# A table of its own for the last batch, and the tail casts of batch 0 on VectorE

## The chip, the cores and the metric

One Trainium2 chip, one of its cores. The metric is the device time of one execution in microseconds, the median of several runs; lower is better.

## The reference

Eight batches, each with 8 heads, 576 positions and 64 values a head. First a retention layer, then a gated layer with a spatial product (all in float32):

```
scores = q @ k^T / 8;  ret = scores * Dmat          # Dmat = gamma_h ** (i - j) for i >= j, else 0
x      = ret @ v                                     # per head; heads side by side: (8, 576, 512)
h      = relu(x @ w_in)                              # w_in 512 x 1024
u, v   = h[..., :512], h[..., 512:]
v_n    = (v - mean(v)) / sqrt(var(v) + 1e-6)
v_s    = einsum('ts,bsd->btd', w_spatial, v_n) + b_spatial[None, :, None]
out    = (u * v_s) @ w_out                           # w_out 512 x 512
```

## The kernel before

**Numbers.** Each fp32 operand of the three large products is kept as a rounded part and a remainder (hi and lo, type fp32r), and a product is three matmuls. ScalarE (ACT) writes hi with a copy or cast, VectorE (DVE) or GpSimd (POOL) writes lo with a subtraction. The weights arrive as 64-bit words and are taken apart by a chain of seven steps: ACT absolute value; maximum on DVE or POOL; shift, high word, low word on DVE, with a PSUM bank as scratch; ACT hi; lo on DVE or POOL.

**Stages.** The 576 positions of a batch are four chunks of 128 and a tail of 64. For each chunk: scores, mask, state update with two decays (dec1 and dec0), and a burst of matmuls that gives a chunk of x. The tail's 64 positions are collected in a tile `xt` and must then be put into the places of the tail in x (`place`). For batches 0 and 1 this is two casts SBUF to SBUF, one for hi and one for lo. From x follow the v half of h with its normalisation (`v`), the u half, the spatial product with the gate, and the output product. Batches 0 and 1 use plain products (`PLAIN = 2`), because the weights are still being made; batches 2 to 7 use a scheme with seven instead of eight products of quarter blocks, whose sums and splits are more DVE, ACT and POOL work.

**Order.** Each engine runs its instructions in program order, and the program order is written out by hand: the tables `ORDER` (start, batches 0 and 1, and the attention of the next ones) and `STEADY` (once for each of the batches 2 to 7, with a, b, c standing for the batch and the two after it; names of batches that don't exist are left out). Each word names a chain, and each time that it stands in the table the chain does its next step. The letters that matter here:

- `w.kind.i.xy` weight block (kind 1: v half of w_in, 0: u half, 2: w_out), maximum on x, lo on y (p POOL, v DVE); `s.n.x` block of w_spatial, lo on x
- `d.b.c`, `D.kind.i`, `T.b`, `S`, `c.x` loads, all issued from the SP queue; `z` a matmul on zeros that only keeps TensorE (PE) busy; `m` two fills on POOL
- `k.b.c.x`, `q.b.c.x` scalings of k and q on x; `g` scores and mask; `p.b.c.xy` state update with dec1 on x and dec0 on y; `b` the burst of a chunk; `t.b.x` and `e.b.x` the tail, prepared and placed on x
- `v.b.n` v half and normalisation of chunk n (4: the tail); a third field says which engine takes the maximum with 0
- `U.t` the first u product of batch 0, 12 matmuls, for columns `t`; `V`, `G`, `X` spatial products and gates; `F` output products
- `W.b.kind.m.part` quarter-block products of batches 2 to 7 (A is three products one after the other in one bank, each copied out by ACT; B two products; C and E one); `R`, `K`, `Y`, `Z` the splits and sums for them

**PSUM.** Four banks are free for all products. Which one a chain takes is read from the string `BANKS`, in order of first use; a chain waits until the last reader of the bank before it is done. The `v` chains of batch 0 keep their bank from the first matmul to the last DVE step of the normalisation. In batches 2 to 7 v lies in the tile `u` in SBUF, and the u half later overwrites its rows.

The steps that the change speaks of:

```
def tail_end(b, eng=po):
    ...
    place_tail(b, eng)          # b < PLAIN: for i in range(2): eng.tensor_copy(out=tail_places(xs[b][:, i]), in_=halves[i])
def decay(t, s, eng=po):
    eng.tensor_tensor(out=t, in0=s, in1=sd.broadcast_to([P, NP, D]), op=ALU.mult)
```

Of the kernel before, what the change touches and what calls it, by code (L numbers as in the profile page):

```python
# [977 lines left out]
```

## Time and profile before

| | us |
|---|---|
| median of 3 runs | 519.97 |
| lowest, highest | 516.78, 521.62 |
| the profiled execution | 519.32 |
| its span, first to last instruction | 517.5 |
| PE busy in the span | 499.2 (96%) |
| DVE, ACT, POOL busy | 403.5, 244.8, 164.6 |

Busy time of PE comes from records in which matmuls overlap, so 96% busy is not 96% of the peak. An engine's idle time matters only where the work that ends last goes through it. Nearly every instruction is recorded under line 166, the helper through which all engines are called, so the rows are told apart by operation and tiles: `out<-in` with buffer numbers left out.

### The profile page before, as it was taken

The numbers are of one execution on the slowest core, as the hardware profiler recorded it, in microseconds if no ns is written. First come the engines' busy times: TensorE is split into PE (matmuls) and PEld (weight loads), VectorE is DVE, ScalarE is ACT, GpSimd is POOL, SyncE is SP. The second block draws the span as 40 slices with busy tenths as digits, with TensorE's granted clock in tenths as the row PEclk, the third lists the DMA queues.
The fourth block names the chain that finished last, engine by engine and source line by source line (L and its number), as shares of the span: only waits on it lengthen the run. The fifth ranks groups of instructions, "written<-read, shape, count | busy, mean of one in ns | idle before, by whom it ended". The sixth has DMA issues, their size and how long they took to land.

```text
span 517.5 us, 16958 instructions
## 1 busy us (share of the span) xinstructions
PE 499.2 (96%) x7323; PEld 471.7 (91%) x7323; DVE 403.5 (78%) x878; ACT 244.8 (47%) x521; POOL 164.6 (32%) x146
## 2 busy tenths in 40 slices
PE   6897999999999999999999999999999999999996
PEld 4676899899999999999999999999999999998996
DVE  3998687997799976788669786888768885877654
ACT  2466516545345462537326472446426472356322
POOL 2796344433016540236014250234213350131010
PEclk9997999999999999999999999999999999999999
DMA  8994343033505522152223442053222420020002
GB/s 282 406 315 164 104 135 116 9 107 103 162 24 156 166 88 84 41 186 84 62 84 106 127 140 80 17 167 129 63 84 67 159 85 1 2 92 1 1 1 92
DMA packets 29949, 55.53 MB, mean 107 GB/s; under 512 B 3249, under 2 KB 15793, under 8 KB 29618
## 3 DMA queue, kind: packets, MB, share of 16 engines
q1 hardware_dynamic: 29874, 54.45, 32.1%
q8 instruction: 57, 0.93, 0.8%
q14 instruction: 18, 0.15, 0.1%
HBM read 45.00 MB, written 9.44 MB: 105 GB/s over the span
## 4 chain that ended last, share of the span: by engine, by line
PE 81%; DVE 10%; DMA 3%; issue 2%; ACT 2%; POOL 1%; SPq 0%; DVEq 0%; ACTq 0%; POOLq 0%
PE m L166 69%; PE r L166 11%; DVE u L166 4%; DMA lent_slot<-in_w_in 2%; DVE slot L166 2%; DVE dec L166 1%; ACT slot L166 1%; DVE m L166 1%; DMA out<-o 1%; ACT u L166 0%; ACT m L166 0%; DVE kn L166 0%; DVE lent_vn L166 0%; POOL room L166 0%; DVE sm L166 0%
## 5 line engine op out<-in xcount | busy, mean ns | idle before, releaser
L166 PE MATMUL m<-wsp,vn 128*128 128x288 f32 x768 | 113.4, 296 | 0.6 <-issue 0.6
L166 PEld LDWEIGHTS m<-wsp,vn 128*128 128x128 f32 x768 | 105.2, 188 | 1.4 <-issue 0.7
L166 DVE TENSOR_TENSOR u<-m,u 128x288 f32<-128x288 f32 (+1 forms) x104 | 45.2, 436 | 21.4 <-PE m L166 12.3
L166 POOL TENSOR_TENSOR slot<-u,slot 128x576 fp32r<-128x576 f32 x8 | 11.5, 1435 | 140.9 <-ACT slot L166 140.9
L166 PE MATMUL m<-slot,win 128*128 128x288 f32 x336 | 53.2, 306 | 2.6 <-DVE vn L166 2.6
L166 PEld LDWEIGHTS m<-slot,win 128*128 128x128 f32 x336 | 49.2, 198 | 3.4 <-POOL wtl L166 3.0
L166 ACT COPY u<-m 128x288 f32<-128x288 f32 (+1 forms) x78 | 28.7, 381 | 32.0 <-PE m L166 26.6
L166 DVE SCALAR_TENSOR_TENSOR u<-u,m 128x288 f32<-128x288 f32 x48 | 21.1, 450 | 28.8 <-PE m L166 28.4
L166 PE MATMUL m<-slot,wout 128*128 128x288 f32 x264 | 39.4, 295 | 0.0
L166 PEld LDWEIGHTS m<-slot,wout 128*128 128x128 f32 x264 | 36.4, 188 | 0.5 <-issue 0.2
L166 PE MATMUL m<-win,slot 128*128 128x512 f32 (+1 forms) x168 | 36.0, 350 | 0.0
L166 ACT CAST slot<-u 128x576 fp32r<-128x576 f32 x32 | 21.5, 674 | 25.8 <-DVE u L166 25.7
L166 ACT COPY r<-warm 1x2 f32<-1x2 f32 x32 | 4.9, 152 | 56.9 <-PE r L166 56.7
L166 PEld LDWEIGHTS m<-win,slot 128*128 128x128 f32 x168 | 26.9, 188 | 4.1
L166 PE MATMUL m<-quarter,slot 128*128 128x256 f32 x216 | 29.9, 283 | 0.5 <-ACT u L166 0.5
L166 POOL TENSOR_TENSOR qk<-qk,qs 128x512 f32<-128x512 f32 (+1 forms) x18 | 23.2, 1286 | 22.4 <-PE r L166 15.1
L166 PE MATMUL m<-slot,part 128*128 128x288 f32 x168 | 27.9, 302 | 2.1 <-ACT o L166 1.5
L166 ACT CAST places<-u 128x576 fp32r<-128x576 f32 x21 | 14.2, 678 | 31.4 <-DVE u L166 31.1
L166 POOL TENSOR_TENSOR kn<-kn,kd 128x512 f32<-128x512 f32 x17 | 17.8, 1048 | 34.1 <-DMA kn<-in_qkv 29.7
L166 PEld LDWEIGHTS m<-quarter,slot 128*128 128x128 f32 x216 | 27.0, 188 | 1.1 <-ACT u L166 0.7
L166 PE MATMUL m<-wtl,vt 128*128 128x288 f32 (+1 forms) x128 | 27.5, 296 | 0.4 <-DVE vt L166 0.4
L166 PEld LDWEIGHTS m<-slot,part 128*128 128x128 f32 x168 | 23.6, 188 | 4.5 <-ACT o L166 2.6
(167 smaller groups left out, 1218.9 us busy)
## 6 DMA issues: line engine op xcount, KB each, us to landing
qk<-in_qkv SPq DMA_DIRECT2D x30, 512.0 KB, 4.3
kn<-in_qkv SPq DMA_DIRECT2D x30, 256.0 KB, 5.0
vv<-in_qkv SPq DMA_DIRECT2D x30, 256.0 KB, 4.4
out<-o SPq DMA_DIRECT2D x32, 144.0 KB, 1.9
tail<-in_tails SPq DMA_DIRECT2D x8, 384.0 KB, 3.3
lent_slot<-in_w_in SPq DMA_DIRECT2D x4, 512.0 KB, 7.0
raw<-in_w_in SPq DMA_DIRECT2D x4, 512.0 KB, 11.5
raw<-in_w_out SPq DMA_DIRECT2D x4, 512.0 KB, 5.9
```

The costliest lines, as they stand in the source:

```text
L166: ins = op(*args, **kw)
```

## The change

- **A third table, `LAST`,** is run for batch 7 in place of `STEADY`. It holds the same steps of batch 7 in another order. The maximum of `v.7.0` goes from DVE to ACT, `Y.7.1` (lo) from DVE to POOL and `Y.7.2` from POOL to DVE.
- **`ORDER`** has the same steps in another order up to about the third chunk of batch 1; from there to its end each engine's order is the old one. These change their engine: `e.0` (the two casts) POOL to DVE; `t.1` and `k.0.2`, `k.1.3`, `q.0.0` POOL to DVE; the maximum of `w.2.1` POOL to DVE; lo of `w.0.1` DVE to POOL; dec1 of `p.0.0` and dec0 of `p.0.0` change places (DVE has dec1); dec0 of `p.0.1` and `p.1.1` DVE to POOL; dec1 of `p.1.0` DVE to POOL. (`e.1` was on DVE before.)
- **`STEADY`** is interleaved anew, with the same steps on the same engines.
- **`BANKS`** is a new string of the same length.

Around the v chains of batch 0, DVE's order before was: v.0.1 statistics steps, dec1 of p.1.0, the four small steps of v.0.2, last step of v.0.1, add of v.0.4, last step of v.0.2. It becomes: the small steps of v.0.1 and v.0.2, last step of v.0.1, the two casts of e.0, add of v.0.4, last step of v.0.2. PE's order there was v.0.4, v.0.3 v0 to v2, b.1.0, v.0.3 v3, U.1, U.0; it becomes v.0.4 and v.0.3 in turns, b.1.0, v.0.3 v2 and v3, U.1, U.0.

The diff, cut to its core:

```
 ORDER = """
-    D.1.1 z.29.1 m c.d z.0.1 c.k z.14.1 d.0.0 z.15.1 c.a d.0.0 z.27.1 d.0.0 z.17.1 c.q z.1.1 z.21.1 z.28.1 z.25.1
-    D.1.3 z.3.1 w.1.1.vp z.13.1 D.1.0 z.7.1 w.1.1.vp d.0.1 d.0.1 g.0.0 d.0.1 g.0.0 D.1.2 k.0.0.v w.1.1.vp d.0.2
...
-    p.0.3.pp S v.0.0 t.0.p t.0.p b.0.2 S v.0.1 w.0.1.pv g.0.3 s.0.p b.0.2 w.0.0.pp p.0.2.pp w.0.1.pv v.0.1 q.0.3.p
...
-    b.0.3 k.1.0.p g.1.0 d.1.2 b.0.3 d.1.1 w.0.2.pv s.4.p D.2.1 v.0.2 s.1.p v.0.0 D.0.3 e.0.p p.1.0.vv e.0.p v.0.2
-    w.0.2.pv s.3.v v.0.4 s.0.p d.1.2 v.0.2 b.0.3 v.0.4 d.1.2 v.0.1 v.0.4 b.0.3 q.1.1.p v.0.4 v.0.1 p.1.0.vv v.0.3
-    v.0.2 p.1.0.vv v.0.3 s.2.p s.5.p v.0.3 v.0.1 v.0.4 e.0.p b.1.0 v.0.2 v.0.3 k.1.1.p v.0.1 v.0.2 v.0.4 U.1 s.5.p
...
+    D.1.1 z.16.1 d.0.0 z.14.1 c.a z.22.1 c.k z.0.1 d.0.0 d.0.0 z.8.1 c.q z.15.1 D.1.3 z.17.1 z.3.1 z.2.1 z.13.1 c.d
+    w.1.1.vp w.1.1.vp w.1.1.vp D.1.0 g.0.0 d.0.1 g.0.0 d.0.1 k.0.0.v d.0.1 D.1.2 p.0.0.vp q.0.0.v d.0.2 w.1.1.vp
...
+    D.2.0 e.0.v k.1.0.p w.0.2.pv v.0.2 s.3.v e.0.v v.0.2 w.0.2.pv s.1.p s.5.p p.1.0.pv w.0.2.pv b.0.3 v.0.4 v.0.2
+    d.1.2 b.0.3 s.0.p s.2.p v.0.3 d.1.2 v.0.2 D.2.1 p.1.0.pv v.0.4 d.1.1 v.0.1 q.1.1.p v.0.2 v.0.3 D.0.3 v.0.2 v.0.4
+    T.1 v.0.1 s.2.p v.0.4 v.0.1 b.1.0 v.0.4 v.0.3 e.0.v v.0.2 p.1.0.pv v.0.3 v.0.4 s.4.p k.1.1.p v.0.2 U.1 v.0.4
+    b.1.0 v.0.4 s.5.p p.1.0.pv U.0 U.1 v.0.4 s.4.p v.0.4 v.0.3 s.3.v b.1.0 g.1.1 b.1.0 d.1.3 p.1.0.pv p.1.1.pp b.1.0
...
+LAST = """
+    W.a.0.0.C W.a.0.0.A W.a.0.1.A W.a.0.0.A W.a.0.0.A W.a.0.1.A W.a.0.0.C W.a.0.1.C W.a.0.0.A W.a.0.0.A W.a.0.1.C
+    W.a.0.0.B W.a.0.0.A W.a.0.0.E W.a.0.0.B W.a.0.0.B W.a.0.0.E v.a.0.a W.a.0.1.A W.a.0.0.B v.a.0.a v.a.2.a v.a.4
+    W.a.0.1.B W.a.0.1.A v.a.2.a v.a.0.a W.a.0.1.A v.a.0.a v.a.2.a v.a.4 W.a.0.1.E v.a.2.a W.a.0.1.A v.a.0.a
+    W.a.1.0.A W.a.0.1.B v.a.2.a v.a.0.a v.a.4 W.a.0.1.E W.a.1.0.A W.a.0.1.B v.a.2.a v.a.1.a v.a.4 W.a.0.1.B
+    W.a.1.0.A v.a.1.a v.a.4 v.a.3.p W.a.1.0.C v.a.4 W.a.1.0.A v.a.1.a W.a.1.0.A v.a.1.a v.a.4 W.a.1.0.B W.a.1.0.C
+    W.a.1.0.A v.a.4 v.a.1.a W.a.1.1.C W.a.1.0.B v.a.4 W.a.1.1.A v.a.1.a v.a.4 W.a.1.0.B W.a.1.1.A W.a.1.1.C
+    W.a.1.1.A v.a.4 v.a.3.p W.a.1.0.E W.a.1.1.A W.a.1.0.B v.a.4 W.a.1.1.B W.a.1.0.E v.a.3.p v.a.3.p W.a.1.1.A v.a.4
+    v.a.3.p W.a.1.1.E v.a.3.p X.a.1.2 W.a.1.1.A X.a.0.2 X.a.1.2 W.a.1.1.B W.a.1.1.E X.a.1.3 X.a.0.0 X.a.1.3 Y.a.3.v
+    Y.a.3.v X.a.0.1 W.a.1.1.B X.a.0.1 X.a.0.0 X.a.0.3 X.a.1.0 X.a.0.3 X.a.0.2 Y.a.2.v Y.a.1.p Y.a.2.v X.a.1.1
+    Y.a.1.p X.a.1.0 W.a.1.1.B W.a.2.0.A X.a.1.1 Z.a.5.vv W.a.2.1.A Z.a.7.vv W.a.2.0.C Z.a.6.vv W.a.2.1.C Z.a.6.vv
+    W.a.2.0.A Z.a.6.vv W.a.2.1.A Z.a.5.vv W.a.2.1.A W.a.2.1.C Z.a.7.vv Z.a.5.vv W.a.2.0.A W.a.2.0.C Z.a.4.vv
+    W.a.2.0.B W.a.2.0.C W.a.2.0.A W.a.2.1.A W.a.2.1.C Z.a.7.vv W.a.2.1.B Z.a.4.vv Z.a.4.vv W.a.2.0.A W.a.2.1.A
+    W.a.2.0.A W.a.2.0.B W.a.2.1.E W.a.2.1.A W.a.2.1.B W.a.2.0.E W.a.2.1.E W.a.2.1.B W.a.2.1.B W.a.2.1.E W.a.2.0.E
+    W.a.2.0.B W.a.2.0.B W.a.2.0.E W.a.2.1.B W.a.2.1.B W.a.2.0.B W.a.2.0.B
+"""
...
     run(ORDER)
-    for b in range(PLAIN, B):
+    for b in range(PLAIN, B - 1):
         run(STEADY, b)
+    run(LAST, B - 1)
```

## Rows read from the trace of the kernel before

**Rows 1.** Windows: busy us (x instructions) by engine, granted clock, DMA share, GB/s.
```profile
12.00:26.00 14.00, 12.19 (x253) 8.12 (x252) 13.30 (x24) 6.08 (x11) 9.51 (x8) 0.88 1.04 406
26.00:44.50 18.50, 18.48 (x362) 14.17 (x362) 17.46 (x35) 13.29 (x27) 18.39 (x19) 1.00 0.98 322
44.50:46.00 1.50, 0.02 (x1) 0.00 (x0) 1.43 (x4) 0.00 (x0) 1.43 (x2) 1.00 0.31 119
46.00:52.80 6.80, 5.68 (x24) 5.71 (x24) 5.04 (x14) 4.12 (x9) 0.75 (x1) 0.50 0.01 4
53.00:120.00 67.00, 66.40 (x1016) 62.03 (x1016) 57.13 (x115) 32.68 (x70) 26.27 (x23) 1.00 0.32 98
...
460.40:485.60 25.20, 22.78 (x172) 21.79 (x171) 19.51 (x55) 14.76 (x32) 1.89 (x2) 1.00 0.08 25
```

**Rows 2.** Timeline of POOL around the first projection: start us, length us, instruction.
```profile
42.06 0.78 POOL L166 CAST slot<-xt 128x256 fp32r<-128x256 f32 x2
42.77 1.08 POOL L166 TENSOR_TENSOR kn<-kn,kd 128x512 f32<-128x512 f32 x1
43.77 1.44 POOL L166 TENSOR_TENSOR wtl<-lent_slot,wtl 64x576 fp32r<-64x576 f32 x1
```

**Rows 3.** Timeline of DVE in the same stretch.
```profile
41.74 3.75 DVE L166 TENSOR_TENSOR dec<-sh,sd 128x256 f32<-128x256 f32 x1
...
46.23 0.74 DVE L166 SCALAR_TENSOR_TENSOR vn<-m,sm,vn 128x512 fp32r<-128x512 f32 x1
```

**Rows 4.** Timeline of PE there; in brackets the idle time before and what ended it.
```profile
43.55 0.96 PE L166 MATMUL m<-win,slot 128*128 128x512 f32 x3
47.12 5.98 PE L166 MATMUL m<-slot,win 128*128 128x288 f32 x24 [2.60 <-DVE vn L166]
```

**Rows 5.** Timeline of PE later: 24 matmuls of the same shape.
```profile
69.99 3.32 PE L166 MATMUL m<-slot,win 128*128 128x288 f32 x24
```

**Rows 6.** Timeline of DVE and POOL around an earlier decay.
```profile
22.91 0.68 DVE L166 TENSOR_TENSOR qsc<-u,qs 128x512 f32<-128x512 f32 x1
23.28 1.47 POOL L166 TENSOR_TENSOR win<-lent_vn,win 128x512 fp32r<-128x512 f32 x1
23.51 1.52 DVE L166 TENSOR_TENSOR dec<-st,sd 128x256 f32<-128x256 f32 x1
```

**Rows 7.** Timeline of DVE and POOL around the tail casts of batch 1.
```profile
94.86 1.59 DVE L166 CAST slot<-xt 128x256 fp32r<-128x256 f32 x2
94.88 1.42 POOL L166 TENSOR_TENSOR x<-win,win 128x512 f32<-128x512 f32 x1
```

**Rows 8.** Instructions on tile xt: least, median and greatest ns; first and last start.
```profile
L166 DVE CAST slot<-xt x2: 276/834/1391, 94.9 to 95.1; 128x256 fp32r<-128x256 f32 x2
```

**Rows 9.** Timeline of DVE: a decay on its own.
```profile
59.65 0.42 DVE L166 TENSOR_TENSOR dec<-st,sd 128x256 f32<-128x256 f32 x1
```

**Rows 10.** Timeline of PE in the last batch, where it waited.
```profile
464.53 1.67 PE L166 MATMUL m<-quarter,slot 128*128 128x256 f32 x12 [0.52 <-ACT u L166]
...
472.29 0.97 PE L166 MATMUL m<-quarter,places 128*128 128x256 f32 x6 [0.92 <-DVE u L166]
...
479.93 0.40 PE L166 MATMUL m<-slot,quarter 128*128 128x288 f32 x1 [0.98 <-ACT u L166]
...
505.33 2.24 PE L166 MATMUL m<-slot,part 128*128 128x288 f32 x12 [0.75 <-ACT o L166]
```

**Rows 11.** Timeline of DVE and ACT in front of the third of these waits.
```profile
478.61 1.37 DVE L166 SCALAR_TENSOR_TENSOR vn<-u,sm,vn 128x512 fp32r<-128x512 f32 x2
...
479.49 0.39 ACT L166 COPY u<-m 128x288 f32<-128x288 f32 x1
```

**Rows 12.** Timeline of DVE at the end.
```profile
501.93 2.34 DVE L166 TENSOR_TENSOR u<-u 128x576 f32<-128x576 f32 x3
...
505.01 0.76 DVE L166 TENSOR_TENSOR slot<-u,slot 128x576 fp32r<-128x576 f32 x1
...
513.96 0.46 DVE L166 TENSOR_TENSOR vl<-m,vl 128x288 f32<-128x288 f32 x1 [0.33 <-PE m L166]
```

More of the change, by code (lines that the diff above doesn't have):

```diff
@@ new lines @@
+    z.7.1 p.0.0.vp w.1.1.vp z.29.1 D.0.0 w.1.3.vv z.27.1 p.0.0.vp d.0.3 z.12.1 w.1.1.vp w.1.3.vv b.0.0 p.0.0.vp
+    z.5.1 w.1.3.vv D.0.1 p.0.0.vp w.1.0.vp z.10.1 m b.0.0 w.1.0.vp b.0.0 b.0.0 w.1.0.vp T.0 q.0.1.p g.0.1 w.1.0.vp
+    b.0.0 c.t z.23.1 w.1.0.vp z.28.1 k.0.1.p z.20.1 d.1.0 w.1.3.vv z.6.1 w.1.0.vp w.1.3.vv w.1.0.vp p.0.1.pp b.0.0 S
+    w.1.2.vp z.11.1 p.0.1.pp w.1.2.vp b.0.1 p.0.1.pp g.0.1 z.4.1 b.0.1 z.30.1 w.1.1.vp w.1.2.vp b.0.1 p.0.1.pp
+    z.21.1 w.1.2.vp z.24.1 p.0.1.pp z.1.1 d.1.0 z.26.1 k.0.2.v z.25.1 g.0.2 w.1.2.vp b.0.1 q.0.2.v d.1.0 w.0.0.pp
@@ new lines @@
+    p.0.2.pp w.1.3.vv z.18.1 w.0.0.pp z.19.1 w.1.2.vp v.0.0 w.1.3.vv b.0.1 g.0.2 v.0.0 w.1.2.vp p.0.2.pp z.9.1 b.0.1
+    v.0.0 D.0.2 w.0.0.pp p.0.2.pp k.0.3.p p.0.2.pp v.0.0 w.0.0.pp S w.0.1.pp b.0.2 g.0.3 p.0.2.pp v.0.0 p.0.3.pp
+    b.0.2 S w.0.1.pp v.0.0 S w.0.0.pp v.0.0 t.0.p t.0.p b.0.2 b.0.2 v.0.1 p.0.3.pp w.0.0.pp w.0.1.pp S q.0.3.p v.0.1
+    t.0.p v.0.0 b.0.2 v.0.1 p.0.3.pp s.0.p b.0.2 v.0.1 q.1.0.p p.0.3.pp d.1.1 w.0.0.pp b.0.3 w.0.1.pp v.0.1 v.0.2
+    g.0.3 b.0.3 v.0.0 v.0.1 b.0.3 d.1.1 w.0.2.pv g.1.0 w.0.1.pp v.0.1 b.0.3 w.0.2.pv d.1.2 g.1.0 s.1.p v.0.2 v.0.0
@@ new lines @@
+    g.1.1 q.1.2.p v.1.0 v.0.4 v.0.3 b.1.1 w.0.1.pp g.1.2 b.1.1 w.0.2.pv p.1.2.vp d.2.0 w.0.3.pp b.1.1 b.1.1 d.1.3
+    g.1.2 v.0.3 w.0.3.pp d.1.3 w.2.0.vv d.2.0 v.0.3 V.0.1 w.2.0.vv p.1.1.pp p.1.2.vp V.1.1 V.0.1 w.0.2.pv p.1.2.vp
+    w.2.0.vv V.0.0 V.1.1 V.0.0 w.2.1.vv V.0.2 k.1.3.v b.1.1 w.2.1.vv w.2.0.vv p.1.2.vp v.1.0 t.1.v V.0.2 p.1.2.vp
+    w.2.0.vv V.1.0 k.2.0.p V.0.0 w.0.3.pp q.1.3.v G.0.1 b.1.1 V.1.0 b.1.2 G.0.1 g.1.3 w.2.1.vv b.1.2 p.1.3.pp
+    w.2.1.vv t.1.v b.1.2 b.1.2 w.2.1.vv G.0.2 w.0.3.pp A.0.1.v w.0.3.pp G.1.1 G.0.2 w.0.3.pp D.2.3 A.0.0.v d.2.0
@@ new lines @@
+    v.1.0 w.0.3.pp p.1.3.pp d.2.1 v.1.0 V.1.2 D.2.2 d.2.1 t.1.v p.1.3.pp v.1.0 A.0.2.v A.0.5.p V.0.3 G.1.1 A.0.3
+    b.1.2 A.0.9.v p.1.3.pp G.0.3 V.0.3 w.2.0.vv A.0.10 w.2.1.vv V.1.3 G.0.3 w.2.0.vv v.1.0 w.2.3.vv G.1.3 g.1.3
+    V.1.3 P.0.1.p b.1.2 w.2.2.pp v.1.1 G.1.3 w.2.1.vv b.1.3 w.2.3.vv g.2.0 b.1.3 V.1.2 b.1.3 P.0.0.v g.2.0 q.2.0.p
+    b.1.3 v.1.0 w.2.3.vv A.0.6.p p.2.0.pv d.2.1 P.0.0.v G.1.2 p.2.0.pv w.2.2.pp b.1.3 w.2.3.vv v.1.0 v.1.1 P.0.1.p
+    G.1.2 v.1.1 w.2.2.pp P.1.1.v F.0.0.1 w.2.3.vv k.2.1.p b.1.3 w.2.2.pp p.2.0.pv e.1.v v.1.1 e.1.v A.0.12.p e.1.v
@@ new lines @@
+    v.1.3 v.1.1 A.0.4.v w.2.3.vv v.1.3 F.0.0.1 A.0.13.v b.2.0 v.1.3 A.1.1.v A.0.14 v.1.3 w.2.2.pp A.0.7 P.1.1.v
+    y.1.2.1 v.1.3 p.2.0.pv P.1.0.v v.1.3 F.0.0.0 A.0.15.v y.1.2.1 b.2.0 v.1.1 A.0.8.v v.1.4 F.0.0.0 v.1.4 v.1.3
+    v.1.3 v.1.4 w.2.2.pp y.1.3.0 P.1.0.v v.1.1 w.2.2.pp v.1.1 g.2.1 w.2.3.vv y.1.3.0 v.1.3 A.0.11.p p.2.1.vv b.2.0
+    v.1.1 v.1.3 b.2.0 d.2.2 v.1.2 v.1.1 T.2 A.1.5.v v.1.2 A.1.0.v v.1.2 v.1.2 y.1.1.1 v.1.2 v.1.2 F.0.0.3 A.1.2.v
+    y.1.1.1 p.2.0.pv A.1.6.v p.2.1.vv v.1.4 F.0.0.3 A.1.9.v F.0.1.3 F.0.0.3 v.1.4 A.1.12.p F.0.0.1 v.1.2 v.1.2
@@ new lines @@
+    F.0.0.0 F.0.1.1 p.2.1.vv F.0.1.3 v.1.4 g.2.1 F.0.0.2 A.1.13.v F.0.1.1 A.1.3 F.0.1.1 v.1.2 d.2.2 A.1.4.v F.0.1.0
+    p.2.1.vv F.0.0.2 q.2.1.v v.1.4 F.0.0.2 A.1.14 v.1.2 y.1.1.0 A.1.15.p v.1.4 F.0.1.0 F.0.1.0 d.2.2 y.1.2.0 y.1.1.0
+    A.1.7 v.1.4 A.1.8.v F.0.1.2 k.2.2.v b.2.0 y.1.3.1 F.0.1.2 A.2.1.v A.2.0.p v.1.4 b.2.1 g.2.2 A.2.2.v b.2.1 v.1.4
+    p.2.2.vv p.2.1.vv q.2.2.p b.2.1 v.1.4 A.2.5.v b.2.1 d.2.3 y.1.3.1 p.2.2.vv d.2.3 v.1.4 X.1.0.2 d.2.3 A.2.6.v
+    F.0.1.2 A.2.9.v F.0.1.3 y.1.0.0 p.2.2.vv A.2.10 g.2.2 y.1.2.0 A.2.12.v A.2.3 b.2.1 y.1.0.1 t.2.v A.2.7 A.1.10
@@ L81 @@
+    y.1.0.0 X.1.0.3 y.1.0.1 k.2.3.v p.2.2.vv A.2.8.v b.2.2 X.1.0.3 g.2.3 p.2.2.vv b.2.2 A.1.11.v t.2.v b.2.2
     p.2.3.vp A.2.4.v d.3.0 b.2.2 A.2.11.v d.3.0 X.1.1.3 d.3.0 A.2.13.v p.2.3.vp X.1.1.2 X.1.1.3 t.2.v X.1.0.2 b.2.2
@@ L113 @@
-"""
-BANKS = "01230123012301230230123010310310230230323130202131030103130303031213121223030303203031231230123013120230102320102012321021201320130312012320102320230103203023102312130230102320102012321021201320130312012320102320230103203023102312130230102320102012321021201320130312012320102320230103203023102312130"
+    b.b.0 W.a.0.1.A b.b.0 d.b.2 W.a.0.1.C p.b.1.vp q.b.1.p d.b.2 W.a.0.0.A d.b.2 g.b.1 p.b.1.vp W.a.0.0.B W.a.0.0.A
+    p.b.1.vp b.b.0 W.a.0.0.E W.a.0.0.B p.b.1.vp v.a.4 W.a.0.0.E W.a.0.0.B v.a.0.v W.a.0.1.A W.a.0.0.B v.a.0.v
@@ new lines @@
+    v.a.2.a W.a.0.1.B W.a.0.1.A v.a.2.a k.b.2.p v.a.4 v.a.0.v W.a.0.1.E v.a.0.v v.a.2.a W.a.0.1.A p.b.1.vp v.a.2.a
+    b.b.1 W.a.0.1.A g.b.2 W.a.0.1.B b.b.1 v.a.0.v p.b.2.pp b.b.1 v.a.0.v b.b.1 d.b.3 W.a.0.1.E W.a.0.1.B d.b.3
+    p.b.2.pp v.a.1.a d.b.3 g.b.2 p.b.2.pp W.a.1.0.A v.a.1.a q.b.2.p v.a.4 W.a.1.0.A W.a.0.1.B v.a.4 b.b.1 p.b.2.pp
+    W.a.1.0.A v.a.4 p.b.2.pp W.a.1.0.C v.a.4 W.a.1.0.A v.a.1.a W.a.1.0.A W.a.1.0.C v.a.4 v.a.1.a W.a.1.1.C v.a.2.a
+    k.b.3.p v.a.4 W.a.1.1.A v.a.1.a v.a.2.a b.b.2 v.a.3.p g.b.3 b.b.2 v.a.1.a v.a.4 p.b.3.vp v.a.4 W.a.1.0.A t.b.p
@@ new lines @@
+    t.b.p b.b.2 W.a.1.1.A b.b.2 q.b.3.p d.c.0 W.a.1.1.C W.a.1.0.B b.b.2 d.c.0 v.a.4 W.a.1.1.A W.a.1.0.B v.a.4
+    v.a.3.p W.a.1.0.E W.a.1.1.A v.a.4 v.a.3.p W.a.1.0.B W.a.1.0.E W.a.1.1.A v.a.3.p W.a.1.1.B W.a.1.0.B v.a.3.p
+    W.a.1.1.E v.a.3.p X.a.0.0 W.a.1.1.A W.a.1.1.B p.b.3.vp W.a.1.1.E p.b.3.vp X.a.0.2 g.b.3 t.b.p p.b.3.vp X.a.0.0
+    X.a.0.1 b.b.3 X.a.0.1 g.c.0 X.a.0.2 b.b.3 b.b.3 b.b.3 d.c.1 d.c.1 X.a.1.3 e.b.v d.c.0 b.b.3 Y.a.1.v e.b.v
+    k.c.0.v W.a.1.1.B X.a.1.3 e.b.v X.a.1.2 q.c.0.v R.b.1.v W.a.1.1.B Y.a.1.v R.b.1.v X.a.0.3 K.b.5.vv X.a.1.2
@@ new lines @@
+    K.b.7.vv Y.a.3.v X.a.1.0 X.a.0.3 Y.a.3.v Y.a.2.p Y.a.2.p X.a.1.1 X.a.1.0 p.c.0.vp X.a.1.1 W.a.2.0.A Z.a.5.vv
+    W.a.2.0.C Z.a.7.vv Z.a.5.vv W.a.2.0.A Z.a.6.vv W.a.2.1.A Z.a.5.vv Z.a.6.vv W.a.2.1.C W.a.2.1.A Z.a.6.vv R.b.2.p
+    W.a.2.1.A Z.a.4.vv Z.a.7.vv R.b.2.p W.a.2.0.C Z.a.4.vv W.a.2.0.A W.a.2.1.C W.a.2.1.A g.c.0 W.a.2.1.C W.a.2.1.B
+    Z.a.7.vv W.a.2.0.C p.c.0.vp W.a.2.0.A W.a.2.0.B d.c.1 Z.a.4.vv W.a.2.1.A p.c.0.vp R.b.3.v W.a.2.0.A R.b.3.v
+    W.a.2.1.A W.a.2.1.E W.a.2.1.B K.b.6.pv W.a.2.0.A p.c.0.vp K.b.5.vv W.a.2.0.B W.a.2.0.B K.b.5.vv K.b.6.pv
@@ new lines @@
+    W.a.2.1.B W.a.2.1.B W.a.2.0.E K.b.4.pv W.a.2.1.B K.b.7.vv W.a.2.0.B W.a.2.1.E W.a.2.0.E W.a.2.1.E W.a.2.0.B
+    W.a.2.1.B p.c.0.vp K.b.4.pv K.b.6.pv W.a.2.0.E W.a.2.0.B K.b.7.vv K.b.4.pv
+"""
+LAST = """
[13 more added lines that the diff above has]
+    W.a.2.0.B W.a.2.0.B W.a.2.0.E W.a.2.1.B W.a.2.1.B W.a.2.0.B W.a.2.0.B
```

53 lines of the change are left out of this document (2 added, 51 removed).

## The prediction

> **What bounds the kernel now.** I read the page first: TensorE (PE) is busy for 96% of the span, so a change can pay only where PE stands idle or runs slowly. Then I cut the span into stretches [rows 1]. From 53 us on PE is busy 66.4 of 67 us, and it stays so through the steady batches. Three places are different. Before 26 us the loads and VectorE's (DVE) weight preparation set the pace. From 44.5 to 52.8 us PE does almost nothing for 1.5 us and then runs at a granted clock of 0.50, the 1.2 GHz level. In the first 25.2 us of the last batch PE is busy for 22.8 us only, because no attention work is left to fill its waits.
>
> The middle place has one cause, found by going from the PE timeline to DVE's and POOL's. Step v3 of `v.0.3` is issued at 43.55, then PE waits 2.60 us, by the trace for DVE writing vn [rows 4]: the first projection U.1 takes the PSUM bank of `v.0.1`, which is free when the last DVE step of that chain ends, 46.23 + 0.74 = 46.97 [rows 3]. That step is late because decay `p.1.0` dec1 stood on DVE from 41.74 for 3.75 us [rows 3]; such an instruction takes 0.42 [rows 9]. In that time POOL ran the two tail casts, a scaling and a subtraction without a break, the last ending at 43.77 + 1.44 = 45.21 [rows 2], and dec1 ended 0.28 later. A smaller case stands at 23.51: 1.52 us behind one POOL subtraction that ended at 24.75 [rows 6]. After the idle time the 24 matmuls of U.1 and U.0 take 5.98 us [rows 4], where 24 of the same shape take 3.32 at the 2.4 GHz level [rows 5].
>
> **The steady batches: nothing.** STEADY is interleaved anew, but read engine by engine each queue has the same order as before, the DMA queue too. The banks of batches 2 to 6 are the old ones renamed (0 with 3, 1 with 2). I cost these five batches at zero; nothing has to hide it.
>
> **The start.** I follow DVE to the last step of `v.0.1`, at 46.97 before. Leaving its queue: dec0 of `p.0.1` (1.52, to POOL) and dec1 of `p.1.0` (3.75, to POOL), together 5.27. Joining it: k.0.2, priced at the 0.68 of q.0.2 beside it [rows 6], and q.0.0, half as wide, priced at the 0.42 of a decay of that width [rows 9]. In `p.0.0` dec1 and dec0 change places between DVE and POOL, which is even. The shift of `w.1.1`, as wide as q.0.2 and so about 0.68, moves into idle time before the first scores. Sum: 46.97 - 5.27 + 0.68 + 0.42 - 0.68 = 42.1. U.1's bank then is free about 2 us before PE, which ends `v.0.3` near 44, could use it.
>
> But U.1 and U.0 read the tail columns of x as well, and the two casts that put them there are now on DVE, right behind that step. On DVE such a cast took 0.276 free and 1.391 blocked [rows 8]; the pair at 94.86 took 1.59 while POOL ran a 1.42 us addition that started 0.02 later [rows 7]. POOL's own row, without the casts (0.78) but with dec1 in their place, still runs back to back and ends about where it did: k.1.1 at 42.77 + 1.08 = 43.85, the subtraction of s.5 at 45.21 [rows 2]. So the casts cost between 0.55 us (end 42.7, hidden, U.1 at 44.0) and a wait for the next gap in POOL's row, as dec1 had it: s.4 follows s.5, as long again, and the casts end near 47.2. If each cast waits for one POOL instruction, they end at 45.21 + 0.15 = 45.4 (the pair at 94.86 ended 0.15 after POOL's addition). I take U.1 at 45.0: by the row of the same casts [rows 7] it would be 44.0, but there POOL had one instruction in their way, and here it has no pause. Queued behind the casts on DVE are the add of `v.0.4` and the last step of `v.0.2`; U.0 (its bank) and V.0.0 wait for these, 1.4 us of DVE work that fits into U.1's own 1.6 us.
>
> The Trainium skill, "SBUF — State Buffer", section "Who interferes with whom", says that a DVE cast can take a port pair shared with GpSimd, and that whoever starts first holds it for the whole instruction. That speaks against putting the casts on DVE here; by it U.1 would start at 45.4, 0.4 us later than in the sum. The rows agree at 94.86; dec1's 3.75 us shows more than one lost turn, which the section does not state.
>
> From U.1 at 45.0 and 24 matmuls at 3.32, U.0 ends at 48.3 instead of 47.12 + 5.98 = 53.1: **4.8 us**. This holds only if the later stages follow. DVE has 67.0 - 57.1 = 9.9 us idle between 53 and 120 [rows 1]; new in its queue there are k.1.3, prep of t.1, the maximum of w.2.1 and the two casts, less the decay dec0 of `p.1.1`, some 1.7 us. The nearest to late is `V.0.0`'s multiply, now behind the w.2.0 steps: by the same durations it ends 1.3 us before G.0.1 needs its bank. If that cover is gone, it costs what exceeds 1.3 us.
>
> **Queues it is moved past.** POOL takes its two memsets after `p.0.0` instead of first; it waits there for loads of the first chunks anyway. The DMA queue puts chunk 1.0 (1,024 KB) ahead of w_in block D.0.2: at 406 GB/s [rows 1] that block lands 2.6 us later; its first reader on ScalarE (ACT) stands six instructions further back. I cost this at zero, with up to 1 us if the reader is early.
>
> **The last batch.** Three PE waits before the u * v_s stage: 0.52 at 464.53 for an ACT copy, 0.92 at 472.29 for DVE, 0.98 at 479.93 for an ACT copy [rows 10], 2.4 us in all against the stretch's 25.2 - 22.8. In each, the next product needs the bank of the one just made and nothing stands between. The last copy was not slow: it ended 0.39 after 479.49 and began when the last step of `v.7.2`, the first of the pair at 478.61, had left the rows it overwrites [rows 11]. LAST puts another product between (0.1.C between A1 and A2 of 0.0.A), takes `v.7.2`'s last step 12 places forward, and moves the maximum of `v.7.0` to ACT. Laying the new order out with these durations (0.70 a product at 256 columns, 0.80 at 288), the first wait goes, the second shrinks to 0.2, the third to about 0.9 spread over the additions: the first X product begins near 483.65 instead of 485.6. Gain 2.0. After it the same chain stands as before: last gate, three subtractions (2.34), cast, subtraction to 505.01 + 0.76 = 505.77 [rows 12], and PE's 0.75 wait at 505.33 with it. It now casts the needed quarter first, for 0.1 more. Y.1's subtraction on POOL (about the 1.42 of the addition in [rows 7]) ends some 0.4 us before the first Z subtraction overwrites its source: covered, at most 1 us if not. The end, from the last addition at 513.96 [rows 12] to the span's 517.5, stays. **2.1 us**, bounds 0 and 3.2 (all of 2.4 and 0.8).
>
> **Sum.** 4.8 + 2.1 = 6.9 us. The profiled execution took 519.32 (span 517.5 and 1.8 around it), 0.65 below the median of 519.97: 512.4 by its own time, 513.1 against the median. One per cent of that, 5.2 us, is about what a measurement of this kernel tells from no change; its three runs span 4.8.
>
> **Rivals**, as medians.
> *POOL's row locks the casts out* as it did dec1, until 47.2; PE idles 3 us, the clock falls to 0.50 again, and the start gives nothing: 519.97 - 2.1 = 517.9. For it: POOL is busy 18.39 of 18.5 us there [rows 1]. Against: blocked DVE instructions elsewhere waited for one POOL instruction [rows 6, 7]. 0.20.
> *The casts wait less, but the clock falls all the same.* Before the fall PE had idled 1.5 us. U.1 at 45.5 and 5.98 us for the two give 51.5: gain 1.6, so 516.3. 0.15.
> *LAST does not do what it says*: its waits move to another copy or bank. 519.97 - 4.8 = 515.2. 0.10.
> *Nothing is left of either wait*: U.1 at 44.0 and all of 3.2 at the end, 511.0. 0.07.
> *The clock is lower through the start*: slower. The idle matmuls that keep PE busy are placed anew, ten instead of thirteen before the first scores. Granted was 0.88 from 12 to 26 us and 1.00 to 44.5 [rows 1]. If it stays at the 1.2 GHz level, the 18.5 us of PE work from 26 on take 37: +18.5 - 6.9, 531.6. It beats the gain from 13.8 us at the low level on. Against it: 20 idle matmuls stand between the first update and v.0.0, 13 before. 0.03.
>
> **How the numbers follow.** The forecast, 513.1, has 0.45, with its own range 511 to 515. Faster by over 1% (below 514.8) are most of it, the better case and part of the third rival, 0.52; within 1% the first two rivals and the rest, 0.45; slower 0.03. The range goes from the better case less the spread of runs to the lock-out plus it: 509.5 to 518.5.
>
> **What would show it.** In the profile after: dec1 of `p.1.0` on POOL near 0.6; no DVE instruction above 1.5 us before 50 us except the casts; U.1 between 44 and 45.5, its 24 matmuls in 3.3 us, granted clock 1.00 from 44 to 53; the period of the steady batches as before; PE idle under 1 us in the last batch before X. The prediction is wrong if the casts end past 46, if 0.50 stands anywhere in 40 to 55 us, or if the lead of 4.8 us at U.0 is lost before 120 us to a wait on V.0.0's bank or on w_out blocks.

## The result, and the profile after

| | median, us | runs | ratio to before, 95% interval |
|---|---|---|---|
| before | 520.6 | 516.78, 521.62, 519.97, 521.22 | |
| after | 513.57 | 514.6, 513.37, 512.59, 513.76 | 0.9879 [0.9833, 0.9925] |

The change gains 6.3 us by the ratio, 3.9 to 8.7 by its interval; 513.1 was forecast. The profiled execution of after took 514.6 us, the slowest of its four. Its two parts share the gain in another way than forecast, so the parts are read first. The page, engines and TensorE's clock:

```profile
span 512.8 us, 16957 instructions
...
PE 499.3 (97%) x7323; PEld 472.8 (92%) x7323; DVE 401.2 (78%) x880; ACT 244.7 (48%) x522; POOL 163.0 (32%) x143
...
PEclk8789999999999999999999999999999999999999
...
q8 instruction: 57, 0.93, 0.7%
```

The windows of after, columns as in [rows 1]; the last row is as long as the last one there and begins just before the last batch's first product (458.62):

```profile
12.00:26.00 14.00, 13.81 (x264) 10.22 (x265) 12.28 (x22) 5.29 (x11) 11.83 (x12) 0.77 1.04 407
26.00:44.50 18.50, 16.36 (x343) 12.80 (x342) 13.71 (x31) 10.18 (x23) 13.31 (x14) 0.91 0.69 221
44.50:52.80 8.30, 8.30 (x148) 7.22 (x148) 6.96 (x20) 5.46 (x13) 6.63 (x6) 1.00 0.85 268
52.80:120.00 67.20, 67.20 (x947) 62.87 (x936) 57.98 (x119) 35.20 (x76) 25.58 (x22) 1.00 0.31 98
...
458.40:483.60 25.20, 25.20 (x193) 24.73 (x193) 20.03 (x57) 15.79 (x34) 2.08 (x2) 1.00 0.07 25
```

The first X product of the last batch, 22.3 us after the first product (25.2 before):

```profile
480.94 0.31 PE L182 MATMUL m<-wsp,vn 128*128 128x288 f32 x1
```

Against [rows 1]: the hole and the half clock at 44.5 to 52.8 are gone, and so are all waits of the last batch ahead of X. But 26 to 44.5, where PE was busy for 18.48 of 18.50 us, now has 2.1 us of idle time and a granted clock of 0.91. The timeline there and at the first projection (in brackets the idle time before, and what ended it; the second column of numbers is the length):

```profile
27.46 0.27 PE L182 MATMUL r<-qsc,sh 64*64 64x64 f32 x1
...
29.14 0.45 PE L182 MATMUL r<-at,u 64*64 64x64 f32 x17
...
31.73 0.55 PE L182 MATMUL r<-at,u 64*64 64x64 f32 x15 [2.13 <-issue]
...
45.79 0.75 DVE L182 SCALAR_TENSOR_TENSOR vn<-m,sm,vn 128x512 fp32r<-128x512 f32 x1
...
46.44 1.65 PE L182 MATMUL m<-win,slot 128*128 128x512 f32 x6
46.45 0.97 DVE L182 CAST slot<-xt 128x256 fp32r<-128x256 f32 x2
46.61 0.66 POOL L182 TENSOR_TENSOR dec<-sh,sd 128x256 f32<-128x256 f32 x1
...
47.93 3.34 PE L182 MATMUL m<-slot,win 128*128 128x288 f32 x24
```

U.1 and U.0 are the 24 matmuls of the last line: 3.34 us at the 2.4 GHz level instead of 5.98 [rows 4], with no wait ahead of them. But U.1 begins at 47.93, not at 45.0, and nothing on DVE holds it: PE itself comes late. The second half of the values products of batch 0, chunk 2 follows the first after 2.13 us in which the trace shows nothing that PE waits for ("issue"); behind it the granted clock is 0.50, the 1.2 GHz level, from 31.96 to 35.37. The windows of these stretches:

```profile
29.60:31.70 2.10, 0.00 (x0) 0.00 (x0) 1.00 (x3) 0.91 (x2) 2.10 (x4) 1.00 1.07 328
31.70:35.40 3.70, 3.67 (x23) 2.88 (x24) 2.90 (x9) 1.16 (x2) 1.83 (x2) 0.54 0.76 210
```

Step by step: after is ahead by 1.84 us at the first V.0.0 product (52.98, before 54.82), by 2.53 at the first X product of batch 1 (125.04 and 127.57), and by 1.78 at PE's wait among the output products of batch 6, 8.4 us ahead of the last batch's first product (450.21 and 451.99). Some of the lead goes at 157 us, where PE waited 0.73 us behind a copy that waited for a store to land; in the profile of before it waited 0.17 there. The last batch then gives 2.7 us. Its end:

```profile
499.80 0.67 ACT L182 CAST slot<-u 128x576 fp32r<-128x576 f32 x1 [4.56 <-DVE u L182]
500.38 0.69 ACT L182 COPY o<-m 128x288 f32<-128x288 f32 x2
...
501.12 1.94 PE L182 MATMUL m<-slot,part 128*128 128x288 f32 x12 [1.02 <-ACT o L182]
...
509.47 0.46 DVE L182 TENSOR_TENSOR vl<-m,vl 128x288 f32<-128x288 f32 x1 [0.34 <-PE m L182]
```

From 450.21 to the end of this last addition (509.93) it is 59.7 us; before, from 451.99 to 514.42 [rows 12], 62.4. The waits of 0.52, 0.92 and 0.98 [rows 10] are gone; the one of 0.75 has become 1.02.

### The profile page after: what moved, and what is told of

Read it like the earlier page. It is cut to its first block, busy times and chain, and to the rows that moved or that the text cites. A ratio compares the mean times of both kernels' runs of the same rounds, so it can differ in the third digit from the quotient of the medians.

```text
span 512.8 us, 16957 instructions
## 1 busy us (share of the span) xinstructions
PE 499.3 (97%) x7323; PEld 472.8 (92%) x7323; DVE 401.2 (78%) x880; ACT 244.7 (48%) x522; POOL 163.0 (32%) x143
## 4 chain that ended last, share of the span: by engine, by line
PE 86%; DVE 7%; issue 2%; DMA 2%; ACT 1%; POOL 1%; SPq 0%; DVEq 0%; ACTq 0%; POOLq 0%
PE m L182 73%; PE r L182 13%; DVE u L182 4%; DVE slot L182 1%; DMA kn<-in_qkv 1%; DMA out<-o 1%; ACT slot L182 1%; DVE kn L182 1%; SPq L182 0%; POOL room L182 0%; DVE x L182 0%; POOL quarter L182 0%; ACT o L182 0%; DVE o L182 0%; DVE sh L182 0%
## 5 line engine op out<-in xcount | busy, mean ns | idle before, releaser
L182 PE MATMUL m<-slot,win 128*128 128x288 f32 x336 | 50.5, 296 | 0.0
L182 POOL TENSOR_TENSOR slot<-u,slot 128x576 fp32r<-128x576 f32 x7 | 10.0, 1429 | 118.0 <-ACT slot L182 118.0
L182 PEld LDWEIGHTS m<-slot,win 128*128 128x128 f32 x336 | 46.7, 188 | 0.5
L182 PE MATMUL m<-win,slot 128*128 128x512 f32 (+1 forms) x168 | 37.2, 359 | 0.0
L182 PEld LDWEIGHTS m<-win,slot 128*128 128x128 f32 x168 | 28.1, 194 | 4.6
L182 PE MATMUL m<-places,wout 128*128 128x288 f32 x168 | 27.1, 298 | 0.7 <-ACT o L182 0.7
L182 POOL TENSOR_TENSOR kn<-kn,kd 128x512 f32<-128x512 f32 x16 | 16.7, 1046 | 27.1 <-DMA kn<-in_qkv 19.0
```

Of the source, the lines that this page charges most:

```text
L182: ins = op(*args, **kw)
```

## The experiments

Twelve kernels ran in three groups, each group on one chip together with before, whose median was 520.9, 520.7 and 520.8 us. Ratios are to before, with 95% intervals.

### Each half alone

```
last_only   tables ORDER and STEADY of before; run(LAST, B - 1) for the last batch
start_only  tables of after, but  for b in range(PLAIN, B): run(STEADY, b)
```

Each has the end of `BANKS` that fits its last table.

last_only: 

> The two halves of the change are independent: with the start of before and the table LAST, PE has no wait above 0.3 us between the start of the last batch's w_in products and the first X product, which comes about 22.3 us after the first w_in product (25.2 before, 22.3 after), and the time is 2.4 to 2.9 us under before: about 517.8 against 520.6. The rival, that the end was only shorter because it met other conditions left by the new start, expects the three waits back (about 2.4 us) and a time within 0.5 us of before.

start_only: 

> With the new start and the last batch run from STEADY as before, the three waits of 0.52, 0.92 and 0.98 us come back. If the wait of 2.14 us at 29.59 and the half clock behind it stand in every execution, the start gives 1.8 us at the first V product and the time is about 518.5; if they stand in the profiled execution alone, the start gives 4 to 5 us and the time is about 516. A wait of instructions (below) stands again after the 17th of the 32 values products of batch 0, chunk 2, or is gone where the packet of instructions came in time; a wait for data could stand only before the first of them.

last_only: 516.54 us, 0.9923 [0.9894, 0.9951]. start_only: 518.16 us, 0.9945 [0.9922, 0.9968]. The windows of last_only, from the first product of the last batch to its first X product:

```profile
460.70:483.05 22.35, 22.35 (x172) 21.89 (x171) 18.59 (x54) 15.39 (x33) 1.91 (x2) 1.00 0.08 28
```

The timeline of PE in start_only, the three waits back:

```profile
462.64 1.67 PE L182 MATMUL m<-quarter,slot 128*128 128x256 f32 x12 [0.52 <-ACT u L182]
470.40 0.98 PE L182 MATMUL m<-quarter,places 128*128 128x256 f32 x6 [0.92 <-DVE u L182]
478.05 1.85 PE L182 MATMUL m<-slot,quarter 128*128 128x288 f32 x12 [0.99 <-ACT u L182]
```

LAST works whatever the start was: 25.2 us [rows 1] become 22.35. Timed, LAST gives 4.0 us (2.6 to 5.5) and the start 2.9 (1.7 to 4.1); the sum, 6.9, agrees with the 6.3 of both. By the profiles, which leave the spread of the start out, LAST's share is 2.7 to 2.8: from the first product of the last batch to its last addition it takes 51.2 to 51.3 us in after and last_only, 54.0 and 54.1 in before and start_only. The 4.0 was more than the 2.4 to 2.9 expected of last_only, though its interval reaches them.

### The wait that no row explains

What is new in after stands at 29.59, and it has the same form in start_only (1.73 us, again after the 17th product) and even in last_only, with the start of before (1.54, there after the 13th). Two edits ask for its cause:

```
values_later   b.0.2 b.0.2 v.0.1 ... v.0.1 ... v.0.1 ... v.0.1   ->   b.0.2 v.0.1 v.0.1 v.0.1 v.0.1 b.0.2 ...
shift_eight    z.13.1   ->   z.13.9      (the tenth idle matmul at the start nine times)
```

values_later: 

> Theory: at 29.59 us PE had run out of instructions. It took 256 of them in 2.1 us (27.47 to 29.59), since only 64x64 products stand there, and the next 16 KB packet of its instruction queue began at 29.22 and ended at 30.16. With the four large product groups of v.0.1 moved between carr0 and the values products, PE has 2.8 us of work in front of the same place: no PE wait above 0.5 us from 27 to 36 us, granted clock 1.00 from 28 to 44 us, U.0 ends between 47.5 and 49.3 us instead of 51.27, time 1.5 to 3.5 us under after, 510 to 512. Rival, a wait for data (tail, mask or values of chunk 2): the 2 us stay in front of the values products, or in front of v.0.1, which now waits in its place; time as after, 513.6.

shift_eight: 

> One idle matmul before the first scores becomes nine: eight more weight loads and eight more matmuls ahead of everything else. If PE runs out of instructions at a fixed count, the wait near 29.6 us moves eight products earlier in the program, to stand after the 9th of the 32 values products instead of the 17th. A wait for data stays after the 17th or goes. The time tells little: 1.7 to 3.4 us of idle matmuls are added where PE waits 2.6 us for the first chunk; 513 to 516.

shift_eight: 514.99 us, 0.9881 [0.9845, 0.9917]. The timeline of PE in shift_eight:

```profile
29.66 0.35 PE L182 MATMUL r<-at,u 64*64 64x64 f32 x9
...
30.75 0.57 PE L182 MATMUL r<-at,u 64*64 64x64 f32 x23 [0.73 <-issue]
```

Eight matmuls more in front, and the break stands after the 9th product instead of the 17th. A window from 0 to a time inside the break counts the PE matmuls up to it (the x behind PE's busy time); in after:

```profile
0.00:30.50 30.50, 25.35 (x476) 18.82 (x476) 22.02 (x42) 11.41 (x22) 16.65 (x21) 0.83 0.97 360
```

and in shift_eight:

```profile
0.00:30.50 30.50, 24.98 (x476) 18.50 (x476) 21.24 (x42) 10.84 (x22) 16.04 (x21) 0.94 0.97 360
```

The count is 476 in both, 476 in start_only, 475 in last_only. The breaks near 60 us of last_only, start_only and others, and before's own at 61.39 (0.6 us), stand after 983 or 984 matmuls, and one in shift_eight after 603. With the weight loads and the few semaphore records of PE's queue (in after 476, 476 and 9) the recorded counts are 961, 1217 and 1985: steps of 256. In the 14 profiles PE has 29 waits that the trace calls "issue", and all of them stand on such a count (705, 961, 1217, 1729, 1985, 4801, 9665). So the break belongs to a number of instructions and not to a datum. The page's row q8 says what comes in such steps: 57 packets, 0.93 MB, 16 KB each, for 14,719 recorded instructions of PE, 258 for each packet. The view of DMA queues of after, cut to 29.1 to 29.4 us (packets, MB, share), has the packet ahead of the break; the trace puts it at 29.22 to 30.15, and none stands in the 5 us before:

```profile
q8 instruction: 1, 0.02, 19.3%
```

PE goes on 1.6 us after this packet has ended, and in all 29 waits a packet ended 1.2 to 1.6 us before PE went on.

The Trainium skill, "Runtime: NRT & Kernel Launch", section "Instruction fetch mechanics", says that an engine fetches its instructions in blocks of 16 KiB (256 of them) through a DMA queue of its own while it executes the block before, and that crossing a boundary is mostly hidden. The trace agrees on the size. It is not hidden here: from 27.47 to 29.59 PE took 256 instructions in 2.1 us, 64x64 products for the most part, and the next block could be executed only from 31.73 on, 4.3 us after the one before was begun. Over the runs this took 2.4 to 7.1 us where PE waited for it. What makes it long was not tested.

values_later: 515.75 us, 0.9914 [0.9889, 0.994], not the 510 to 512 expected. The break was gone, but PE waited 2.12 us from 34.01 on for DVE's remainder of chunk 2, which follows the values products, and the granted clock fell to 0.50 behind that wait too (36.55 to 39.96). The timeline of PE there:

```profile
33.31 0.69 PE L181 MATMUL r<-at,u 64*64 64x64 f32 x32
36.12 0.24 PE L181 MATMUL r<-qsc,sh 64*64 64x64 f32 x1 [2.12 <-DVE slot L181]
```

The wait did not come where the rival had it, in front of the values products or of v.0.1, but behind the values products: with these moved back, DVE stood idle for 2.47 us ahead of the tail's mask, which comes right behind them (34.14; in after 32.39), and all of its queue behind that came later.

### Which of the two moves makes the gain of the start

```
dec_pool    before, p.1.0.vv -> p.1.0.pv                     casts_dve   before, e.0.p -> e.0.v
pair_only   before, both                                     both_back   after, both undone
```

dec_pool: 

> Kernel before with one edit: decay dec1 of p.1.0 on POOL. If the 3.75 us of that decay on VectorE were what held v.0.1, its last step ends 2 to 4 us earlier where the block stood, U.1 begins near 45, and the time is 2 to 4.8 us under before, 516 to 519 against 520.9. The rival, that PE itself arrives late in most executions (v.0.3's last group at 46 to 48 us in the four runs above, 43.55 in the profile of before), expects less than 1 us.

casts_dve: 

> Kernel before with one edit: the tail casts of batch 0 on VectorE, the decay left on VectorE. Lost turns: POOL's row is shorter by 0.8 us but still without a pause, so the decay, and the casts after it in VectorE's queue, wait until a gap in the row; U.1 within 0.7 us of 47.1 and a time within 1 us of before. If the casts on POOL were the cause of the block, the decay takes under 1.5 us, and the time falls by 2 us or more.

pair_only: 

> Kernel before with both edits and nothing else of the new order: if the two moves make the gain of the start, the time is as with the new start alone, 0.9945 of before or less, about 518; if the rest of the new order makes it, within 1 us of before. The casts, behind the decay on POOL as in the changed kernel, take 1 us if the first of them begins before the decay and 2 to 3 us if it begins after it.

both_back: 

> The changed kernel with both moves undone (casts on POOL, decay on VectorE), all else as changed. If the moves make the gain of the start, 2 to 4 us over the changed kernel: ratio to before 0.993 to 0.996, about 517 to 519, with VectorE's decay standing over 2 us beside POOL's row. If the order makes it, the ratio is that of the changed kernel, 0.988, about 514.5.

| kernel | decay dec1 / casts on | median, us | ratio, 95% interval |
|---|---|---|---|
| dec_pool | POOL / POOL, old order | 517.38 | 0.9925 [0.9895, 0.9955] |
| casts_dve | DVE / DVE, old order | 520.95 | 1.0 [0.9973, 1.0028] |
| pair_only | POOL / DVE, old order | 517.19 | 0.9941 [0.9916, 0.9965] |
| both_back | DVE / POOL, new order, LAST | 513.66 | 0.9866 [0.9848, 0.9884] |

In the old order the decay alone gives what both moves give; the casts on DVE give nothing, and where pair_only met POOL's row they took 1.88 us:

```profile
45.06 1.88 DVE L166 CAST slot<-xt 128x256 fp32r<-128x256 f32 x2
```

U.1 did not begin near 45 in dec_pool, as expected, but at 47.50, without a wait and at the full clock; in casts_dve it began at 49.55, not within 0.7 of 47.1. In the new order neither move is needed. The timeline of DVE in both_back:

```profile
42.82 0.75 DVE L182 SCALAR_TENSOR_TENSOR vn<-m,sm,vn 128x512 fp32r<-128x512 f32 x1
43.49 0.47 DVE L182 TENSOR_TENSOR dec<-sh,sd 128x256 f32<-128x256 f32 x1
```

The first line is the last step of v.0.1. Before, the decay stood ahead of it [rows 3]; the new ORDER has it behind, so a blocked decay could not hold U.1's bank on either engine. That it is this place which makes the move needless is read from these lines; no run changed the place alone. Of the two cases that I had named for both_back, the one in which the moves make the gain was wrong by 3 us or more; the one in which the order makes it came.

The profile of before shows the block of 3.75 us. In last_only and casts_dve, which keep the decay on DVE in the old order, it took 0.51 and 0.41; there PE had stopped for instructions (1.54 us in both), the clock had fallen, and POOL's row had a gap of 0.8 and 1.4 us when the decay's turn came. In casts_dve:

```profile
46.96 0.41 DVE L166 TENSOR_TENSOR dec<-sh,sd 128x256 f32<-128x256 f32 x1
```

How often an execution of before goes the one way or the other, a profile of one execution can't tell. The mean granted clocks of the runs go with the gain: 0.9875 over the 49 runs of before in the three groups and 0.988 in casts_dve, against 0.991 in dec_pool, pair_only and start_only and 0.994 in both_back. So less time at the half clock is likely a part of what the start gains; how large a part was not tested.

What the casts do behind the decay is seen in shift_eight, where PE came earlier than in after. DVE and POOL there:

```profile
44.26 0.61 POOL L182 TENSOR_TENSOR dec<-sh,sd 128x256 f32<-128x256 f32 x1
44.59 3.02 DVE L182 CAST slot<-xt 128x256 fp32r<-128x256 f32 x2
44.84 1.05 POOL L182 TENSOR_TENSOR kn<-kn,kd 128x512 f32<-128x512 f32 x1
45.84 3.07 POOL L182 TENSOR_TENSOR wtl<-lent_slot,wtl 64x576 fp32r<-64x576 f32 x2
...
47.47 0.73 PE L182 MATMUL m<-slot,win 128*128 128x288 f32 x3 [0.69 <-DVE slot L182]
```

The casts begin 0.33 us after the decay on POOL. The first waits through the rest of it and through two instructions more, until the gap between the two subtractions (47.25 to 47.33); the pair ends at 47.61, and U.1 waits for the first of them, which ends at 47.41. In after and start_only the first cast began 0.15 us before the decay, and the pair took 0.97. So the rival of the lock-out is real, at 2 us more for the pair, and a few tenths decide whether it comes.

### Without the break

```
cut_after   after;  nine of the first ten idle matmuls z.n.1 -> z.n.4, each four matmuls of 128 columns
cut_back    both_back with the same cut
cut_copies  cut_back;  LAST: Z.a.6.vv W.a.2.0.A Z.a.6.vv W.a.2.1.A  ->  W.a.2.0.A W.a.2.1.A Z.a.6.vv Z.a.6.vv
```

after_again: 

> The changed kernel, unaltered, as the mark for the three beside it and as a second profile of its start: 0.986 to 0.990 of before, and a PE wait of 1 to 2.2 us without a releaser after the same count of PE instructions (961 recorded) as in its first profile.

cut_after: 

> Nine of the ten idle matmuls at the start are each cut into four of 128 columns: the same columns, 27 matmuls and 27 weight loads more, so every boundary of 256 PE instructions falls 54 instructions earlier in the program. By the times between the same instructions in the run start_only, the blocks that PE emptied in 2.1 and 3.0 us then hold work for 5.5 and 5.2 us, above the 3.6 to 4.5 us that a new block took to come in the runs so far. Theory: no wait without a releaser between 25 and 62 us, and a time 1.5 to 3 us under the unaltered kernel beside it. Rival, that VectorE and POOL set the arrival of U.1 anyway: the waits go, others for DVE or POOL take their place, and the time is within 0.7 us of it.

cut_back: 

> The same cut in the kernel with both moves undone (casts on POOL, decay on VectorE behind the last step of v.0.1). With PE earlier by the stalls, the casts on VectorE would meet POOL's row (2 to 3 us in two of the runs above); on POOL they cannot. So if casts become the bound, this one is faster than the kernel with the cut alone by 0.5 to 2 us; if they don't, it is the same within 0.7 us.

cut_copies: 

> As the one before, and in LAST the two copies of the first w_out products (0.A and 1.A, A0) are put ahead of the cast of the difference Z.6 in ScalarE's queue. The wait of 1.02 us before A1 of 1.A in the last batch ended with the second of these copies, which stood behind that cast; it should shrink to 0.3 to 0.5, as A1 then waits for the cast alone. Gain 0.4 to 0.7 us, seen in the profile; in the times hardly above their uncertainty.

| kernel | median, us | ratio, 95% interval |
|---|---|---|
| after_again | 514.15 | 0.9869 [0.9845, 0.9893] |
| cut_after | 515.15 | 0.9885 [0.9861, 0.9909] |
| cut_back | 515.02 | 0.989 [0.9868, 0.9912] |
| cut_copies | 516.16 | 0.99 [0.9876, 0.9924] |

The break came again in after_again, as expected, after the recorded count 961. PE's waits from 25 to 125 us there (us in all, times, longest):

```profile
PE r L182 <- issue: 1.7, 1, 1.7
PE m L182 <- issue: 0.5, 1, 0.5
PE m L182 <- POOL win L182: 0.2, 1, 0.2
```

and in cut_after:

```profile
PE r L182 <- issue: 0.3, 1, 0.3
```

Of the breaks 0.3 us is left in cut_after, and no granted clock below 1.00 stands there from 19.85 us, where its records begin, to 511.37, 0.4 us before the end. PE goes on behind it 5.5 us after the block before was begun, longer than the 3.6 to 4.5 that I had counted on. The cut did not end the breaks for good: from 25 to 125 us cut_back has 1.0 us of them and cut_copies 2.0, the longest of 1.08 at the count 1729. From the first burst product of chunk 2 (b.0.2) to U.1 it takes 16.75 us (30.83 to 47.58), in after_again 20.05 (26.58 to 46.63). So the break and the half clock behind it cost about 3.3 us in this stretch; the stop of 1.70 and half of the 3.41 us at the half clock make 3.4. The time did not follow, as the cut was dear elsewhere; PE's timeline in cut_after begins:

```profile
1.50 8.47 PE L182 MATMUL m<-wsp 128*128 128x128 f32 x37 [1.50 <-DVE wsp L182]
```

and in after_again:

```profile
1.50 4.63 PE L182 MATMUL m<-wsp 128*128 128x512 f32 x10 [1.50 <-DVE wsp L182]
```

37 small matmuls take 8.47 us, 0.23 each, where I had counted a quarter of 0.46: the first scores come 3.6 us later, and b.0.2 4.25. The two nearly cancel: 515.15 against 514.15, with intervals that overlap, so neither the gain of 1.5 to 3 us that I expected nor a time within 0.7 us. In cut_back the casts were not the bound (515.02 against 515.15). cut_copies shrank the wait of 1.02 to 0.41, but PE then waited 0.40 after the first matmul, for the difference itself:

```profile
503.12 0.40 PE L182 MATMUL m<-slot,part 128*128 128x288 f32 x1 [0.41 <-ACT slot L182]
503.91 1.74 PE L182 MATMUL m<-slot,part 128*128 128x288 f32 x11 [0.40 <-DVE slot L182]
```

Its last batch gained nothing: 51.3 us from the first product to the last addition, as in cut_back. None of the kernels beats the changed one by more than its uncertainty; both_back equals it.

## Why the prediction was right, and where it was not

**The steady batches.** As forecast: from X of batch 2 to X of batch 6 it takes 237.4 us before and 237.45 after, and the lead at 125 us reaches the last batch less what the store at 157 takes. Of the twelve other profiles eight, of both orders, have that wait of PE (0.55 to 1.27); in before it is 0.17.

**The last batch.** The mechanism is the forecast one; the term was mis-sized: 2.7 us instead of 2.1, inside its bounds of 0 and 3.2. I left 0.2 and 0.9 of the second and third wait in the sum; all three are gone (X begins 30.7 us after the opening wait, 33.6 before: 2.9). What comes back behind X is 0.2, where I had 0.1: the wait of 0.75 became 1.02, ended by a copy that stands behind the cast in ACT's queue.

**The start.** Forecast 4.8; the time says 2.9 (1.7 to 4.1) for the new start alone, the profile of after 1.84 at the first V product and 2.53 at 125 us, and after_again 3.1 there. Two steps failed. The first is the sum of what leaves DVE's queue, "dec1 of `p.1.0` (3.75, to POOL)": as both_back shows, the new order has this gain without the move, and by the trace it is the new place of that decay, behind the last step of v.0.1, that gives it. In the old order the move to POOL alone does give 3.9 us (2.3 to 5.5), so that v.0.1 should not stand behind this decay was right. The end of that sum, 42.1 for the last step of v.0.1, came at 46.54 in after (45.79 + 0.75): it took whole durations off a queue that itself waits for PE, for 1.79 us ahead of the tail's mask alone. The second is the time of U.1, "near 44" for PE and 45.0 for the casts: I let PE run on as it had in the profile of before, 18.48 of 18.50 us busy [rows 1]. With the values products closed up behind the scores, update and tail scores, PE empties 256 instructions in 2.1 us and stops; v.0.3's last group began at 47.24 instead of 43.55. Of the marks that I named, the casts ended past 46 (47.42): by this one the account of the start was wrong, though the time came out. No 0.50 stood in 40 to 55 us; it stood at 32 to 35.4, where I had not looked. The lead at U.0 was not lost later; it grew up to 125 us.

**The rivals.** The lock-out did not set the end in after, but it did in shift_eight. "The clock falls all the same" happened in after, behind another wait and earlier. The slower rival did not come as a whole: 0.50 was granted for 10.24 us from 8.06 on and for 3.41 from 31.96 on. The first of these cost little: after_again, which has no 0.50 on record from 7.73 to 31.62, waits in that stretch for ACT, POOL and DVE instead (1.17, 0.80 and 0.51 us) and begins b.0.2 0.9 us earlier (26.58 against 27.46). That the sum came out right was in part luck, two errors of opposite sign: by its own timing the start gave 1.9 us less than forecast, by the profiles the end gave 0.6 more.

## What to carry to other kernels

A wait of PE that no semaphore explains should be counted in instructions before it is sought in data: put a few idle matmuls in front and see whether it moves. Mixing runs of small matmuls with large ones, so that a block of 256 instructions lasts longer than the next takes to come, removed the wait in values_later; neither there nor in cut_after did the time gain, as other costs took its place. And a block of an instruction by a neighbour engine may be cured more surely by what stands behind it in the queue than by the engine that executes it: undo the move in the new order before the move gets the credit.

## What the hardware showed

PE's instructions come in packets of 16 KB, 256 of them. PE stopped at the recorded counts 705, 961, 1217, 1729, 1985, 4801 or 9665, all of them a multiple of 256 apart, under four different orders of its work (old, new, with eight matmuls more, with the cut); the stops without a releaser lasted 0.17 to 2.13 us, and each ended 1.2 to 1.6 us after a packet.

After such a stop the granted clock fell to 0.50 for 3.41 us in after (stop 2.13), after_again (1.70), last_only and casts_dve (1.54 each), and did not in start_only (1.73), both_back (1.11) and shift_eight (0.73): the length of the stop alone does not decide.

A cast on DVE that came 0.33 us after POOL's instruction took 2.82 us instead of 0.28, two further POOL instructions included; the decay of [rows 3] took 3.75 us in the same way. The Trainium skill, "SBUF — State Buffer", section "Who interferes with whom", has the lock for one instruction; the runs show that the waiting side can lose several turns while the other's row has no gap.

An idle matmul of 128 columns took 0.23 us at the start of cut_after, as against 0.46 for one of 512 columns at the start of after_again: half as long, not a quarter. The granted clock of these stretches is not on record (it begins at 19.85 and 7.73 us), so a part of this can be the clock.
